# Scores of two heads in float32 on TensorE's row halves, with no split of q and k, and a list schedule that knows the ports shared by VectorE and GpSimd

## The chip, the core and the metric

The kernel runs on one core of one Trainium2 chip. The metric is the device time of one execution in microseconds; less is better. A core has five engines with a queue each: TensorE (PE; its weight loads are shown as PEld), VectorE (DVE), ScalarE (ACT), GpSimd (POOL) and SyncE (SP), which issues the DMAs here.

## What is computed

Sliding-window attention with a linear bias, and behind it a feed-forward part on the attention's output.

```python
# q, k, v: (8 batches, 8 heads, 576 positions, 64)
scores = scale * np.matmul(q, k.transpose(0, 1, 3, 2))
rel = pos[:, None] - pos[None, :]
mask = (rel >= 0) & (rel < 128)
scores = np.where(mask, scores - slopes[h] * np.abs(rel), -1e9)
attn = softmax(scores)
x = (attn @ v).transpose(0, 2, 1, 3).reshape(4608, 512)
h = x @ w_in                                   # 512 -> 2048
g = h * erf(softplus(h))
out = g @ w_out                                # 2048 -> 512
```

Results are wanted at about float32 accuracy. The kernel multiplies some operands as float32 (in the trace one such matmul is two instructions) and others in the rounded type fp32r (one instruction); where fp32r is used, an operand is split into a high and a low part and several products are added.

## The kernel before

**Attention.** There are 32 pairs of heads (8 batches, 4 pairs of heads each). The query positions of a pair are cut into five tiles of 128 (`QTILES`), which see 128, 256, 256, 256 and 192 keys. A "span" is a run of tiles with one load of q and k: tiles 0 to 2, or tiles 3 and 4, and in the later batches both follow from one load. `operands` (L386) loads q and k. `parts` (L439) makes from them what the fp32r products need: for each of the two heads a scaled and rounded k in both row halves (`kh`, L451 on VectorE or L453 on ScalarE), its rest (`kl`, L463, VectorE), the rounded q in the head's own half (`a`, L472 or L474), and q's rest in the other half (L466, GpSimd). So one product of 128 rows adds q-high and q-low at once, and a tile of one head is `a·kh + a·kl`, two fp32r matmuls (L511). The first four spans (`EARLY`) take another way, `early_parts`: q is scaled alone (L435), and each head is one float32 matmul on 64 of the 128 rows (L497).

After the scores, for each tile: VectorE adds the bias and takes the row minimum of the negated scores (L522), ScalarE takes the exponential with its sum (L532), VectorE inverts the sums (L549, L550), GpSimd scales (L560), TensorE transposes by a matmul with the identity (L578), ScalarE or VectorE copies (L472, L474), TensorE multiplies with v in float32 (L596), and the result is copied and stored to DRAM as a chunk of x.

**Feed-forward.** x is cut into 12 chunks of 384 tokens, w_in and w_out into 16 slices of 128 hidden units. A first pass takes slices 0 to 5 over all chunks, beside attention; a second takes the other ten, and adds what the first stored. `Weights.prepare` makes float32 high and low parts out of the weights' 64-bit words (L670 to L692: ScalarE, VectorE and GpSimd). `load_x` splits a chunk (L766 or L768, L759). `unit` (one slice with one chunk) runs 12 fp32r matmuls into a PSUM bank "h" (L782) and copies it out as `hs` (L766, L768); `flush` takes softplus and erf (L811, L813), the product with h (L824) and its split (`gh`; `gl`, L829); `products` runs nine fp32r matmuls into three banks "o" (L844).

**PSUM.** Eight banks: "h" two, "o0" to "o2", and attention's "s", "t" and one for the products with v. One bank "s" holds both heads of a tile.

**The order.** It is made ahead of the run by a list scheduler (`Plan.run`). Each piece of work is an `op` with a cost in us per engine that may do it, the buffers that it reads and writes, and a due time `at`. When an engine is free in the plan, it takes the ready op of the lowest `(at, seq)` whose buffers are to be had. An op that several engines may do goes to the one that ends it first. The order so found is each engine's queue; on the chip each engine runs its queue in order and waits on semaphores, so the planned costs (`dve`, `act`, `pool_tt`, `pool_ts`, `fp32_us`, `f32r_us`) set the order and nothing else. Forty float32 matmuls of no use (`warm_up`, L383) fill TensorE's free time at the start, with the latest due time of all.

Of the kernel before, what the change touches and what calls it, by code (L numbers as in the profile page):

```python
# [8 lines left out]
F32 = mybir.dt.float32  # L9
# [4 lines left out]
ALU = mybir.AluOpType  # L14
# [19 lines left out]
EARLY = 4  # L34
# [6 lines left out]
PB, XB, OB, TB, TBB = 8, 3, 3, 2, 2  # L41
BT = 0
# [90 lines left out]
class Plan:  # L133
# [16 lines left out]
    def op(self, costs, emit, r=(), w=(), at=0.0, moved=0, rows=1.0):  # L150
        o = Op()
        o.rows = rows
# [31 lines left out]
    def run(self):  # L184
# [6 lines left out]
        transfer = 0.0  # L191
# [48 lines left out]
        while events:  # L240
# [17 lines left out]
            for e in ("SP", "PE", "Act", "DVE", "Pool"):  # L258
                while free.get(e, 0.0) <= t + 1e-9 and ready.get(e):
                    best = None  # L260
                    for o in ready[e]:
                        if o.ready > t + self.WAIT[e] + 1e-9 or (best and (best.at, best.seq) < (o.at, o.seq)):
                            continue
                        if fits(o) and all(t + o.costs[e] <= max(free[x], t) + c for x, c in o.costs.items()):
                            best = o
# [36 lines left out]
def dve(n, fast=False):  # L302
    return 0.17 + n * (0.00056 if fast else 0.00108)


def act(n, aps=0, src=0.15):
# [36 lines left out]
class Attention:  # L343


    def __init__(self, tc, plan, ctx, actx, qT, kT, vb, bias, ident, moe):
# [5 lines left out]
        self.raw, self.split, self.pp, self.ptp, self.xsb = (  # L352
            sb(n) for n in ("raw", "split", "pp", "ptp", "xsb")
        )
# [10 lines left out]
        self.seq = 0  # L365
# [20 lines left out]
    def operands(self, i, w=None):  # L386

        nc, op = self.nc, self.plan.op
        sync = nc.sync.dma_start
        b, g = self.order[i]  # L390
        at = step_time(self.step) - LL
        q0, q1 = (0, S) if w is None else SPANS[w][1:3]
        k0 = max(0, q0 - WIN)
        nq, nk = q1 - q0, q1 - k0
        early = self.seq < EARLY
        nm = f"{i}_{w}"
        tags = [("a0", "kh0"), ("a1", "kh1"), ("kl0", "kl1")][self.seq // 2 % 3]
        self.seq += 1
        if early:
            q = Buf(self.split, [P, S], F32, tags[0], 2, "a" + nm)  # L400
            k = Buf(self.split, [P, S], F32, tags[1], 2, "k" + nm)
            op(emit=lambda e: sync(k[:, :nk], self.kT[b, g, :, k0:q1]), w=[k], at=at, **dma(P * nk * 4))
        else:
            q = Buf(self.raw, [P, S], F32, "qr", 1, "qr" + nm)
            k = Buf(self.raw, [P, 2, S], F32, "kr", 1, "kr" + nm)
            src = self.kT[b, g, :, k0:q1].rearrange("(j d) s -> d j s", j=2)

            def both(e):
                for half in range(2):
                    sync(k[half * D : (half + 1) * D, :, :nk], src)  # L410

            op(emit=both, w=[k], at=at, **dma(2 * P * nk * 4, 2, 0.65))
        op(emit=lambda e: sync(q[:, :nq], self.qT[b, g, :, q0:q1]), w=[q], at=at, **dma(P * nq * 4))
        at = step_time(self.step) - LP
        return (*(self.early_parts if early else self.parts)(nm, g, q, k, nq, nk, at), q0, k0)
# [16 lines left out]
    def early_parts(self, nm, g, q, k, nq, nk, at):  # L432
        for j in range(2):
            rows = slice(j * D, (j + 1) * D)
            self.plan.op({"DVE": dve(nq, True)}, lambda e, j=j, rows=rows: self.nc.vector.tensor_scalar(  # L435
                q[rows, :nq], q[rows, :nq], 2.0 ** (2 * g + j), None, op0=ALU.mult), r=[q], w=[q], at=at)
        return q, k, None

    def parts(self, nm, g, q, k, nq, nk, at):  # L439

        nc, op = self.nc, self.plan.op
        lo, hi = slice(0, D), slice(D, P)
        a = [Buf(self.split, [P, S], F32R, f"a{j}", 2, f"a{nm}_{j}") for j in range(2)]
        kh = [Buf(self.split, [P, S], F32R, f"kh{j}", 2, f"kh{nm}_{j}") for j in range(2)]
        kl = [Buf(self.split, [P, S], F32R, f"kl{j}", 2, f"kl{nm}_{j}") for j in range(2)]

        def scaled(e, out, src, by):
            if e == "DVE":  # L450
                nc.vector.tensor_scalar(out, src, by, None, op0=ALU.mult)  # L451
            else:
                nc.scalar.mul(out, src, by)  # L453

        either = lambda n: {"DVE": dve(n, True), "Act": act(n)}
        for j in range(2):
            own, other = (lo, hi) if j == 0 else (hi, lo)
            by = 2.0 ** (2 * g + j)
            op(either(nk), lambda e, j=j, by=by: scaled(e, kh[j][:, :nk], k[:, j, :nk], by),
               r=[k], w=[kh[j]], at=at)  # L460
            op(either(nq), lambda e, j=j, own=own: self.copy(e, a[j][own, :nq], q[own, :nq]),
               r=[q], w=[a[j]], at=at)
            op({"DVE": dve(nk)}, lambda e, j=j, by=by: nc.vector.scalar_tensor_tensor(  # L463
                kl[j][:, :nk], k[:, j, :nk], by, kh[j][:, :nk], op0=ALU.mult, op1=SUB),
                r=[k, kh[j]], w=[kl[j]], at=at)
            op({"Pool": pool_tt(nq)}, lambda e, j=j, own=own, other=other: nc.gpsimd.tensor_tensor(  # L466
                a[j][other, :nq], q[own, :nq], a[j][own, :nq], SUB), r=[q, a[j]], w=[a[j]], at=at)
        return a, kh, kl

# [6 lines left out]
    def scores(self, i, t, operands, low, total, at):  # L476
# [5 lines left out]
        a, kh, kl, q0, k0 = operands  # L482
        k0 = start - WIN + c0 * 64 - k0
        q0 = start - q0
        src = []
        if kl is None:

            ways = [((self.ps, "s", 1), (self.ps, "t", 1))]
            if i < NPAIR and t < 3:
                ways = [((self.ps, "s", 1), (self.spare[1], "o0", 1)), ((self.spare[0], "h", 2),) * 2]  # L490
            for j, (pool, tag, bufs) in enumerate(ways[self.step % len(ways)]):
                src.append((Buf(pool, [P, 2, 256], F32, tag, bufs, f"s{i}_{t}_{j}"), 0))

            def products(e):
                for j in range(2):
                    rows = slice(j * D, (j + 1) * D)
                    nc.tensor.matmul(  # L497
                        src[j][0][:m, src[j][1], :n], lhsT=a[rows, q0 : q0 + m],
                        rhs=kh[rows, k0 : k0 + n], start=True, stop=True,
                    )  # L500

            op({"PE": 2 * fp32_us(n) + 0.05}, products, r=[a, kh], w=[src[0][0], src[1][0]],
               at=at, rows=0.5)
        else:
            ps = Buf(self.ps, [P, 2, 256], F32, "s", 1, f"s{i}_{t}")
            src = [(ps, 0), (ps, 1)]

            def products(e):
                for j in range(2):
                    for o, rhs in enumerate((kh[j], kl[j])):  # L510
                        nc.tensor.matmul(  # L511
                            ps[:m, j, :n], lhsT=a[j][:, q0 : q0 + m], rhs=rhs[:, k0 : k0 + n],
                            start=(o == 0), stop=(o == 1),
                        )

            op({"PE": 4 * f32r_us(n) + 0.05}, products, r=[*a, *kh, *kl], w=[ps], at=at)
# [3 lines left out]
        def biased(e):  # L520
            for j in range(2):
                nc.vector.tensor_tensor_reduce(  # L522
                    out=pt[:m, c0:c1, j, :], in0=blocks(src[j][0][:m, src[j][1], :n]),
# [17 lines left out]
    def normalise(self, i, ts, p, st, totals, at):  # L541
# [11 lines left out]
        op({"DVE": 0.5}, inverse, r=sums, w=sums, at=at)  # L553
# [13 lines left out]
    def transpose_bank(self, i, w, bi, p, sb, at):  # L567
# [18 lines left out]
        op({"DVE": dve(width), "Act": act(width, src=0.13)},  # L586
# [18 lines left out]
    def span(self, i, w, operands, v):  # L605
# [32 lines left out]
        op({"DVE": dve(n), "Act": act(n, src=0.13)},  # L638
# [7 lines left out]
class Weights:  # L646
# [9 lines left out]
    def prepare(self, which, f, at, after=()):  # L656
# [27 lines left out]
        for fast, dst, emit in steps:  # L684
            op({"DVE": dve(DM, fast)}, lambda e, emit=emit: emit(), r=[raw, q, t], w=[dst], at=at)
# [4 lines left out]
            r=[t, *after], w=[hi], at=at)  # L690
        op({"Pool": pool_tt(DM), **({"DVE": dve(DM)} if WLO else {})}, lambda e: (
            nc.gpsimd if e == "Pool" else nc.vector).tensor_tensor(lo.all, flt(t), hi.all, SUB),  # L692
            r=[t, hi, *after], w=[lo], at=at)
# [3 lines left out]
class Moe:  # L697
# [42 lines left out]
    def load_x(self, c, first, at):  # L740
# [11 lines left out]
        for k2 in range(2):  # L752
# [4 lines left out]
               lambda e, hi=hi, src=src: self.copy(e, hi.all, raw[:, src]), r=halves[k2], w=[hi], at=at - XS)  # L757
            op({"Pool": pool_tt(2 * CH), **({"DVE": dve(2 * CH)} if XLO else {})},
               lambda e, hi=hi, lo=lo, src=src: (nc.vector if e == "DVE" else nc.gpsimd).tensor_tensor(  # L759
                   lo.all, raw[:, src], hi.all, SUB), r=[*halves[k2], hi], w=[lo], at=at - XS)  # L760
# [9 lines left out]
    def unit(self, c, f, w, x, po, start, end, first, at):  # L770
# [3 lines left out]
        ps = Buf(self.ps_h, [P, 512], F32, "h", 2, f"h{U}")  # L774
# [16 lines left out]
        op({"Act": act(CH, src=0.13), "DVE": dve(CH)},  # L791
# [3 lines left out]
    def flush(self):  # L795
# [23 lines left out]
        for us, n, n2, hs, s, at in pairs:  # L819
# [5 lines left out]
                r=[s, hs], w=[hs], at=at)  # L825
# [142 lines left out]
```

## Time and profile before

| what | us |
|---|---|
| median of three runs (lowest, highest) | 1118.45 (1116.33, 1119.25) |
| the profiled execution | 1118.25 |
| its span, first to last instruction | 1116.3 |

In the page's line of busy time, a share is of the span. Matmuls are pipelined: a record's length holds the way through the array, so from one start to the next is the better measure of what a matmul costs, and a busy TensorE is not a TensorE at its peak. "PEclk" is the clock that TensorE was granted, in tenths; in this profile it is low only in the first slices, where TensorE has idle time. In a list of groups, the first number after the bar is busy time in us, the second the mean of one in ns, and what follows the second bar is the engine's idle time just before, with what ended it.

### The profile page before, as it was taken

How to read it: one execution, taken by the hardware profiler on the slowest of the kernel's cores; microseconds unless marked ns; L12 is line 12 of the kernel's file. 1: busy time of each engine (PE TensorE's matmuls, PEld its weight loads, DVE VectorE, ACT ScalarE, POOL GpSimd, SP SyncE). 2: the span in 40 equal slices, each digit the busy share in tenths (PEclk: the TensorE clock that was granted, in tenths of full speed). 3: DMA queues.
4: the chain of work that ended last, by engine and by line, in shares of the span. 5: the costliest groups of instructions: out<-in, count | busy, mean ns of one | idle time of the engine just before them, and what ended most of it. 6: DMA issues, size and time to landing. Idle time of an engine off the chain costs nothing.

```text
span 1116.3 us, 17069 instructions
## 1 busy us (share of the span) xinstructions
PE 1073.7 (96%) x6000; PEld 976.5 (87%) x6000; DVE 684.9 (61%) x1602; ACT 721.9 (65%) x1436; POOL 385.7 (35%) x464
## 2 busy tenths in 40 slices
PE   9776979999999999999999999999999999999998
PEld 8666968988899999999899998899999999999996
DVE  5878898887888888775867675333433433433332
ACT  6567667878788787776677675355455455455462
POOL 5776887646666566653333231000000000000000
PEclk9797999999999999999999999999999999999999
DMA  6444555444545455422343422202202202202102
GB/s 184 139 132 122 140 152 153 146 132 115 163 118 135 121 143 149 118 89 78 114 132 114 141 69 74 86 13 73 85 19 67 85 19 67 85 13 73 57 19 67
DMA packets 89732, 111.59 MB, mean 100 GB/s; under 512 B 45744, under 2 KB 59696, under 8 KB 89648
## 3 DMA queue, kind: packets, MB, share of 16 engines
q1 hardware_dynamic: 89648, 110.52, 33.5%
q8 instruction: 47, 0.77, 0.3%
q14 instruction: 37, 0.30, 0.1%
HBM read 82.18 MB, written 28.31 MB: 99 GB/s over the span
## 4 chain that ended last, share of the span: by engine, by line
PE 82%; DVE 9%; POOL 3%; DMA 2%; issue 2%; ACT 2%; POOLq 0%; SPq 0%; DVEq 0%; ACTq 0%
PE o L844 32%; PE h L782 31%; PE px L596 7%; PE s L511 5%; PE t L578 5%; POOL p L560 2%; DMA xr<-xd 2%; DVE p L522 1%; PE warm_ps L383 1%; DVE xl L759 1%; POOL wto L686 1%; DVE hs L824 1%; DVE gl L829 1%; PE s L497 1%; ACT p L532 1%
## 5 line engine op out<-in xcount | busy, mean ns | idle before, releaser
L782 PE MATMUL h<-xh,whi 128*128 128x384 f32 x768 | 262.5, 342 | 0.0
L782 PE MATMUL h<-xl,whi 128*128 128x384 f32 x768 | 259.2, 338 | 1.6 <-DVE xl L759 1.6
L782 PE MATMUL h<-xh,wli 128*128 128x384 f32 x768 | 259.7, 338 | 0.0
L560 POOL TENSOR_SCALAR p<-p,st 128x256 f32<-128x256 f32 (+2 forms) x320 | 194.0, 623 | 128.1 <-DVE st L550 108.1
L844 PE MATMUL o<-who,gh 128*128 128x512 f32 x576 | 228.8, 397 | 0.6 <-DVE ot L768 0.6
L844 PE MATMUL o<-who,gl 128*128 128x512 f32 x576 | 227.6, 395 | 1.2 <-DVE gl L829 1.2
L844 PE MATMUL o<-wlo,gh 128*128 128x512 f32 x576 | 227.3, 395 | 1.2 <-POOL wlo L692 0.7
L766 ACT COPY hs<-h 128x384 f32<-128x384 f32 x137 | 65.3, 477 | 215.1 <-PE h L782 214.6
L532 ACT ACTIVATE p<-p,st 128x256 f32<-128x256 f32 (+2 forms) x320 | 149.0, 468 | 24.5 <-DVE st L522 23.6
L782 PEld LDWEIGHTS h<-xl,whi 128*128 128x128 f32 x768 | 145.2, 189 | 8.7 <-DVE xl L759 2.1
L782 PEld LDWEIGHTS h<-xh,whi 128*128 128x128 f32 x768 | 145.3, 189 | 6.9 <-ACT hs L766 0.2
L782 PEld LDWEIGHTS h<-xh,wli 128*128 128x128 f32 x768 | 144.8, 189 | 0.2 <-POOL wli L692 0.2
L844 PEld LDWEIGHTS o<-who,gl 128*128 128x128 f32 x576 | 108.1, 188 | 25.4 <-DVE gl L829 2.1
L522 DVE CUSTOM_DVE_ANT_0 p<-s,bias_sb 128x256 f32<-128x256 f32 (+2 forms) x320 | 109.4, 378 | 33.4 <-PE s L511 21.6
L768 DVE COPY hs<-h 128x384 f32<-128x384 f32 x55 | 30.4, 554 | 160.8 <-PE h L782 160.8
L844 PEld LDWEIGHTS o<-wlo,gh 128*128 128x128 f32 x576 | 108.5, 188 | 17.9 <-POOL wlo L692 2.2
L844 PEld LDWEIGHTS o<-who,gh 128*128 128x128 f32 x576 | 108.6, 188 | 16.6 <-DVE ot L768 1.5
L824 DVE TENSOR_TENSOR hs<-s,hs 128x768 f32<-128x768 f32 x96 | 95.2, 1016 | 23.4 <-ACT s L813 23.4
L829 DVE TENSOR_TENSOR gl<-hs,gh 128x768 fp32r<-128x768 f32 x96 | 94.6, 989 | 15.5 <-ACT gh L766 14.7
L578 PE MATMUL t<-ident,p 128*128 128x128 f32 x544 | 85.7, 284 | 17.6 <-POOL p L560 11.8
L578 PEld LDWEIGHTS t<-ident,p 128*128 128x128 f32 x544 | 65.6, 147 | 30.4 <-POOL p L560 14.6
L466 POOL TENSOR_TENSOR a_None<-qr_None,a_None 64x576 fp32r<-64x576 f32 x48 | 76.4, 1592 | 25.7 <-DVE a_None L474 20.7
(80 smaller groups left out, 1653.1 us busy)
## 6 DMA issues: line engine op xcount, KB each, us to landing
xr<-xd SPq DMA_DIRECT2D x22, 768.0 KB, 4.3
kr_None<-k_t SPq DMA_DIRECT2D x48, 288.0 KB, 4.2
pd<-ot SPq DMA_DIRECT2D x36, 256.0 KB, 3.7
ot<-pd SPq DMA_DIRECT2D x36, 256.0 KB, 3.0
wri<-w_in SPq DMA_DIRECT2D x16, 512.0 KB, 3.8
wro<-w_out SPq DMA_DIRECT2D x16, 512.0 KB, 3.7
out_dram<-ot SPq DMA_DIRECT2D x32, 256.0 KB, 2.1
qr_None<-q_t SPq DMA_DIRECT2D x24, 288.0 KB, 3.1
```

The source lines that it names most:

```text
L466: op({"Pool": pool_tt(nq)}, lambda e, j=j, own=own, other=other: nc.gpsimd.tensor_tensor(a[j][other, :nq], q[own, :nq], a[j][own, :nq], SU ...
L511: nc.tensor.matmul(ps[:m, j, :n], lhsT=a[j][:, q0 : q0 + m], rhs=rhs[:, k0 : k0 + n], start=(o == 0), stop=(o == 1),)
L522: nc.vector.tensor_tensor_reduce(out=pt[:m, c0:c1, j, :], in0=blocks(src[j][0][:m, src[j][1], :n]), in1=blocks(self.bias[:m, c0 * 64 : c1 ...
L532: nc.scalar.activation(dst, dst, AF.Exp, bias=low[:m, j : j + 1], scale=-1.0, accum_out=total[:m, j : j + 1],)
L560: nc.gpsimd.tensor_scalar(dst, dst, totals[t][:m, j : j + 1], 1.0, op0=ALU.mult, op1=ALU.mult)
L578: nc.tensor.matmul(ps[:, col : col + P], lhsT=p[t][:, kb].rearrange("p j d -> p (j d)"), rhs=self.ident[:, :], is_transpose=True, start=no ...
L596: self.nc.tensor.matmul(dst[:, q0 - base : q1 - base], lhsT=v[:, blk], rhs=sb[sbi][:, off : off + q1 - q0], start=(blk == order[0][0]), st ...
L766: self.nc.scalar.copy(out, src)
L782: nc.tensor.matmul(ps[:, :CH], lhsT=ww[:, cs], rhs=xx[:, k], start=(k2 + k + n == 0), stop=(k2 + k + n == 4),)
L824: V if e == "DVE" else G).tensor_tensor(hs[:, :n], s[:, :n], hs[:, :n], ALU.mult),
L829: V if e == "DVE" else G).tensor_tensor(gl[:, :n], hs[:, :n], gh[:, :n], SUB),
L844: nc.tensor.matmul(po.all, lhsT=g[:, j, cs], rhs=w.all, start=(u["start"] and n == 0), stop=(u["end"] and n == 2),)
```

## The change

Scores: `EARLY`, `early_parts` and `parts` go. Every span loads q and k once, keeps them in float32 (three buffers each), and scales q in one VectorE instruction, by a column `heads` (1 in the first 64 rows, 2 in the others) and by 4^g. Each tile is two float32 matmuls, one head on rows 0 to 63, the other on rows 64 to 127, each into a PSUM bank of its own.

PSUM: attention's "s" has two banks, "h" has one.

Scheduler: an op has a set `shares` of engines on which it uses the ports that VectorE and GpSimd share; all GpSimd work is in it, and VectorE work that is marked `both=True`. In the plan no two of them overlap, and VectorE leaves the turn to a ready GpSimd op with an earlier due time. VectorE is asked a second time after GpSimd. The planned costs have new constants.

```diff
@@ Plan @@
+    def op(self, costs, emit, r=(), w=(), at=0.0, moved=0, rows=1.0, both=False):
+        o.shares = {"Pool", "DVE"} if both else {"Pool"}
...
-            for e in ("SP", "PE", "Act", "DVE", "Pool"):
+            def first(e):
+                best = None
+                for o in ready[e]:
+                    if o.ready > t + self.WAIT[e] + 1e-9 or (best and (best.at, best.seq) < (o.at, o.seq)):
+                        continue
+                    if e in o.shares and ports > t + 1e-9:
+                        continue
+                    if fits(o) and all(t + o.costs[e] <= max(free[x], t) + c for x, c in o.costs.items()):
+                        best = o
+                return best
+            for e in ("SP", "PE", "Act", "DVE", "Pool", "DVE"):
...
+                    if e == "DVE" and e in best.shares and free.get("Pool", 0.0) <= t + 1e-9 and ready.get("Pool"):
+                        other = first("Pool")
+                        if other and other.ready <= t + 1e-9 and (other.at, other.seq) < (best.at, best.seq):
+                            break
...
+                    if e in best.shares:
+                        ports = best.end
@@ planned costs @@
-    return 0.17 + n * (0.00056 if fast else 0.00108)      # dve
+    return 0.14 + n * (0.00054 if fast else 0.00108)
-    return src + 0.093 * aps + n * 0.000833               # act, src 0.15
+    return src + 0.093 * aps + n * 0.00088                # src 0.17
-    return 0.15 + n * 0.0025                              # pool_tt
+    return 0.18 + n * 0.00214
-    return 0.36 + n * 0.00135                             # pool_ts
+    return 0.27 + n * 0.00082
@@ Attention @@
+        self.heads = Buf(sb("heads"), [P, 1], F32, "heads", 1, "heads")
+        for j in range(2):
+            plan.op({"Pool": 0.2}, lambda e, j=j: self.nc.gpsimd.memset(
+                self.heads[j * D : (j + 1) * D], 2.0**j), w=[self.heads], at=-1)
...
+        q = Buf(self.split, [P, S], F32, "q", QB, "q" + nm)
+        k = Buf(self.split, [P, S], F32, "k", QB, "k" + nm)
+        op({"DVE": dve(nq, True)}, lambda e: nc.vector.tensor_scalar(
+            q[:, :nq], q[:, :nq], self.heads[:, 0:1], 4.0**g, op0=ALU.mult, op1=ALU.mult),
+           r=[q, self.heads], w=[q], at=step_time(self.step) - LP, both=True)
-    def early_parts(self, nm, g, q, k, nq, nk, at):
...
-    def parts(self, nm, g, q, k, nq, nk, at):
...
+        ways = [((self.ps, "s", 2),) * 2]
+        if i < NPAIR and t < 3:
+            ways.append(((self.spare[0], "h", 1), (self.spare[1], "o0", 1)))
...
+        def products(e):
+            for j in range(2):
+                rows = slice(j * D, (j + 1) * D)
+                nc.tensor.matmul(
+                    src[j][0][:m, :n], lhsT=q[rows, q0 : q0 + m], rhs=k[rows, k0 : k0 + n],
+                    start=True, stop=True,
+                )
+        op({"PE": 2 * max(n / 1200.0, 0.205) + 0.15}, products, r=[q, k], w=[x[0] for x in src],
+           at=at, rows=0.8)
@@ Moe.unit @@
-        ps = Buf(self.ps_h, [P, 512], F32, "h", 2, f"h{U}")
+        ps = Buf(self.ps_h, [P, 512], F32, "h", 1, f"h{U}")
```

Marked `both=True` are, besides the scaling of q: the inversion of the sums, VectorE's steps in `Weights.prepare`, the split of x, and in `flush` the product with h and the two parts of g.

More of the change, by code (lines that the diff above doesn't have):

```diff
@@ L33 @@
 TAIL = (2, 2)
-EARLY = 4
 DIRECT = 2
@@ L41 @@
 PB, XB, OB, TB, TBB = 8, 3, 3, 2, 2
+QB = 3
 BT = 0
@@ L190, in run @@
         events = []
-        transfer = 0.0
+        transfer = ports = 0.0
         key = lambda b: (id(b.pool), b.tag)
@@ L257, in run @@
                         enable(x, max(late, t))
-            for e in ("SP", "PE", "Act", "DVE", "Pool"):
-                while free.get(e, 0.0) <= t + 1e-9 and ready.get(e):
[L260 to L265, printed above, removed]
+            def first(e):
[9 more added lines that the diff above has]
+            for e in ("SP", "PE", "Act", "DVE", "Pool", "DVE"):
+                while free.get(e, 0.0) <= t + 1e-9 and ready.get(e):
+                    best = first(e)
                     if best is None or best.ready > t + 1e-9:
                         break
+                    if e == "DVE" and e in best.shares and free.get("Pool", 0.0) <= t + 1e-9 and ready.get("Pool"):
+                        other = first("Pool")
+                        if other and other.ready <= t + 1e-9 and (other.at, other.seq) < (best.at, best.seq):
+                            break
                     for x in best.costs:
@@ L351, in __init__ @@
         ps = lambda name: ctx.enter_context(tc.tile_pool(name=name, bufs=1, space=PSUM))
-        self.raw, self.split, self.pp, self.ptp, self.xsb = (
-            sb(n) for n in ("raw", "split", "pp", "ptp", "xsb")
-        )
+        self.split, self.pp, self.ptp, self.xsb = (sb(n) for n in ("split", "pp", "ptp", "xsb"))
         self.ps = ps("ps_a")
@@ L394, in operands @@
         nq, nk = q1 - q0, q1 - k0
-        early = self.seq < EARLY
         nm = f"{i}_{w}"
[L397 to L412, printed above, removed]
+        q = Buf(self.split, [P, S], F32, "q", QB, "q" + nm)
+        k = Buf(self.split, [P, S], F32, "k", QB, "k" + nm)
+        op(emit=lambda e: sync(k[:, :nk], self.kT[b, g, :, k0:q1]), w=[k], at=at, **dma(P * nk * 4))
         op(emit=lambda e: sync(q[:, :nq], self.qT[b, g, :, q0:q1]), w=[q], at=at, **dma(P * nq * 4))
-        at = step_time(self.step) - LP
-        return (*(self.early_parts if early else self.parts)(nm, g, q, k, nq, nk, at), q0, k0)
+        op({"DVE": dve(nq, True)}, lambda e: nc.vector.tensor_scalar(
+            q[:, :nq], q[:, :nq], self.heads[:, 0:1], 4.0**g, op0=ALU.mult, op1=ALU.mult),
+           r=[q, self.heads], w=[q], at=step_time(self.step) - LP, both=True)
+        return q, k, q0, k0
     def values(self, i, c0, c1):
@@ L430, in values @@
         return v
-    def early_parts(self, nm, g, q, k, nq, nk, at):
[L433 to L437, printed above, removed]
-    def parts(self, nm, g, q, k, nq, nk, at):
[L443 to L468, printed above, removed]
     def copy(self, e, out, src):
@@ L481, in scores @@
         n = (c1 - c0) * 64
-        a, kh, kl, q0, k0 = operands
+        q, k, q0, k0 = operands
         k0 = start - WIN + c0 * 64 - k0
         q0 = start - q0
[L485 to L516, printed above, removed]
@@ new lines, in scores @@
+        ways = [((self.ps, "s", 2),) * 2]
+        if i < NPAIR and t < 3:
+            ways.append(((self.spare[0], "h", 1), (self.spare[1], "o0", 1)))
+        src = [
+            (Buf(pool, [P, 512], F32, tag, bufs, f"s{i}_{t}_{j}"), 0)
+            for j, (pool, tag, bufs) in enumerate(ways[self.step % len(ways)])
+        ]
+        def products(e):
[5 more added lines that the diff above has]
+                )
@@ L552, in normalise @@
         sums = [totals[t] for t in ts]
-        op({"DVE": 0.5}, inverse, r=sums, w=sums, at=at)
+        op({"DVE": 0.42}, inverse, r=sums, w=sums, at=at, both=True)
         for t in ts:
@@ L637, in span @@
             xs = Buf(self.xsb, [P, n], F32, f"xs{w}", 1, f"xs{i}_{w}")
-        op({"DVE": dve(n), "Act": act(n, src=0.13)},
+        op({"DVE": dve(n), "Act": act(n, src=0.145)},
            lambda e: self.copy(e, xs.all, px[:, :n]), r=[px], w=[xs], at=at + 0.1)
@@ L684, in prepare @@
         for fast, dst, emit in steps:
-            op({"DVE": dve(DM, fast)}, lambda e, emit=emit: emit(), r=[raw, q, t], w=[dst], at=at)
+            op({"DVE": dve(DM, fast)}, lambda e, emit=emit: emit(), r=[raw, q, t], w=[dst], at=at, both=True)
         op({"Pool": pool_tt(DM)}, lambda e: nc.gpsimd.tensor_tensor(flt(t), flt(t), flt(q), ALU.add),
@@ L689, in prepare @@
             nc.scalar.copy if e == "Act" else nc.vector.tensor_copy)(hi.all, flt(t)),
-            r=[t, *after], w=[hi], at=at)
+            r=[t, *after], w=[hi], at=at, both=True)
         op({"Pool": pool_tt(DM), **({"DVE": dve(DM)} if WLO else {})}, lambda e: (
             nc.gpsimd if e == "Pool" else nc.vector).tensor_tensor(lo.all, flt(t), hi.all, SUB),
-            r=[t, hi, *after], w=[lo], at=at)
+            r=[t, hi, *after], w=[lo], at=at, both=True)
         self.t[which, f] = (hi, lo)
@@ L756, in load_x @@
             op({"DVE": dve(2 * CH, True), "Act": act(2 * CH)},
-               lambda e, hi=hi, src=src: self.copy(e, hi.all, raw[:, src]), r=halves[k2], w=[hi], at=at - XS)
+               lambda e, hi=hi, src=src: self.copy(e, hi.all, raw[:, src]), r=halves[k2], w=[hi], at=at - XS, both=True)
             op({"Pool": pool_tt(2 * CH), **({"DVE": dve(2 * CH)} if XLO else {})},
                lambda e, hi=hi, lo=lo, src=src: (nc.vector if e == "DVE" else nc.gpsimd).tensor_tensor(
-                   lo.all, raw[:, src], hi.all, SUB), r=[*halves[k2], hi], w=[lo], at=at - XS)
+                   lo.all, raw[:, src], hi.all, SUB), r=[*halves[k2], hi], w=[lo], at=at - XS, both=True)
             x.append((hi, lo))
@@ L790, in unit @@
         hs, half = self.hs, len(self.round) % 2
-        op({"Act": act(CH, src=0.13), "DVE": dve(CH)},
+        op({"Act": act(CH, src=0.145), "DVE": dve(CH)},
            lambda e: self.copy(e, hs[:, half], ps[:, :CH]), r=[ps], w=[hs], at=at)
@@ L858, in store @@
         if u["first"]:
-            op({"DVE": dve(DM), "Act": act(DM, src=0.13)},
+            op({"DVE": dve(DM), "Act": act(DM, src=0.145)},
                lambda e: self.copy(e, ot.all, po.all), r=[po], w=[ot], at=at)
```

14 lines of the change are left out of this document (6 added, 8 removed).

## The prediction

> **What bounds the kernel now.** I read the page's busy shares first, then its 40 slices and the chain, then the windows by stage, and only then single groups and the order of time on TensorE.
>
> ```profile
> PE 1073.7 (96%) x6000; PEld 976.5 (87%) x6000; DVE 684.9 (61%) x1602; ACT 721.9 (65%) x1436; POOL 385.7 (35%) x464
> PEclk9797999999999999999999999999999999999999
> PE 82%; DVE 9%; POOL 3%; DMA 2%; issue 2%; ACT 2%; POOLq 0%; SPq 0%; DVEq 0%; ACTq 0%
> 20.00:200.00 180.00, 149.72 (x884) 135.58 (x884) 151.02 (x423) 123.71 (x331) 135.68 (x157) 0.90 0.52 143
> 200.00:520.00 320.00, 315.01 (x2041) 292.70 (x2039) 251.13 (x763) 255.10 (x648) 186.72 (x249) 1.00 0.44 125
> 600.00:1117.00 517.00, 511.45 (x2560) 462.10 (x2558) 211.76 (x281) 277.40 (x350) 27.80 (x20) 1.00 0.19 63
> ```
>
> The window columns are busy time of PE, PEld, DVE, ACT, POOL, then the granted clock. TensorE carries 82% of the chain, but not evenly. From 20 to 200 us it is busy 149.7 of 180 us, idle 30.3, at a granted clock of 0.90; VectorE is busy 151.0 (84%), ScalarE 123.7 (69%), GpSimd 135.7 (75%). From 200 to 520 us TensorE is busy 315.0 of 320 at full clock. After 600 us there is only the feed-forward part, and TensorE is never free. So work taken from the other engines pays before 200 us; work given to TensorE costs after 200 us. The change does both, and the forecast is their difference.
>
> **The change part by part.** Times are made against the profiled execution, 1118.25 us (span 1116.3, about 2 us around it); the median of the three runs, 1118.45, is 0.2 above.
>
> *1. The splits of q and k go.* These groups, all between 20 and 200 us, fall away:
>
> ```profile
> L463 DVE SCALAR_TENSOR_TENSOR kl<-kr,kh 128x320 fp32r<-128x320 f32 (+1 forms) x22 | 11.6, 547 | 1.9 <-ACT kh L453 1.8
> L463 DVE SCALAR_TENSOR_TENSOR kl_None<-kr_None,kh_None 128x576 fp32r<-128x576 f32 x10 | 7.9, 792 | 0.0
> L451 DVE TENSOR_SCALAR kh<-kr 128x320 fp32r<-128x320 f32 (+1 forms) x14 | 6.5, 492 | 1.8 <-DMA kr<-k_t 1.8
> L451 DVE TENSOR_SCALAR kh_None<-kr_None 128x576 fp32r<-128x576 f32 x5 | 3.1, 625 | 0.2 <-PE s L511 0.2
> L474 DVE CAST a<-qr 64x192 fp32r<-64x192 f32 (+1 forms) x11 | 4.6, 421 | 3.3 <-DMA qr<-q_t 3.2
> L474 DVE CAST a_None<-qr_None 64x576 fp32r<-64x576 f32 x7 | 3.9, 558 | 0.0
> L453 ACT ACTIVATE kh<-kr 128x320 fp32r<-128x320 f32 x8 | 3.5, 466 | 2.1 <-PE s L511 1.7 <-DMA kr<-k_t 0.4
> L453 ACT ACTIVATE kh_None<-kr_None 128x576 fp32r<-128x576 f32 x5 | 3.4, 673 | 0.0
> L472 ACT CAST a<-qr 64x192 fp32r<-64x192 f32 (+1 forms) x11 | 4.3, 394 | 1.1 <-DMA qr<-q_t 1.0
> L472 ACT CAST a_None<-qr_None 64x576 fp32r<-64x576 f32 x3 | 2.0, 672 | 0.1
> L466 POOL TENSOR_TENSOR a<-qr,a 64x192 fp32r<-64x192 f32 (+1 forms) x24 | 22.5, 936 | 13.5 <-DVE wqi L678 4.2 <-DVE a L474 3.1 <-ACT a L472 2.2
> L466 POOL TENSOR_TENSOR a_None<-qr_None,a_None 64x576 fp32r<-64x576 f32 x10 | 16.3, 1632 | 3.1 <-DVE a_None L474 2.5
> ```
>
> VectorE loses 11.6+7.9+6.5+3.1+4.6+3.9 = 37.6 us, ScalarE 3.5+3.4+4.3+2.0 = 13.2, GpSimd 22.5+16.3 = 38.8. Added is one VectorE scaling of q per span. GpSimd's 34 instructions were two a span, so 17 spans; at about 0.45 us (the casts of q took 0.42 to 0.56 on half the partitions) that is 7.7 us. VectorE goes from 151.0 to 121.1, ScalarE from 123.7 to 110.5, GpSimd to 96.9. Many copies may run on VectorE or ScalarE, and the planner hands them out, so I take the two together: 274.7 becomes 231.6, a factor 0.843. If they stay as loaded as now, the stage takes 0.843 × 180 = 152 us: **28 us** less. VectorE alone would give 144, ScalarE alone 161, which are the inner bounds. TensorE's floor is about 141: 149.7 us of busy time at clock 0.90 is 135 at full clock, and part 2 adds some 6. Then 39 us would be gained; nothing gained is the other end, if the stage is a chain of waits and not a load.
>
> The second load of k (two transfers become one) leaves the SP queue and is costed at nothing: no transfer stands on the chain for more than the 2% named above.
>
> *2. Scores as two float32 products on row halves.* The first four spans of before already do exactly this, at L497, so the price is in the trace.
>
> ```profile
> 14.52 1.14 PE L497 MATMUL s<-k,a 64*128 64x256 f32 x8
> 15.59 1.16 PE L383 MATMUL warm_ps<-warm 128*128 128x128 f32 x8
> 17.77 0.49 PE L497 MATMUL s<-k,a 64*128 64x128 f32 x4
> 18.19 1.96 PE L596 MATMUL px<-pa,vbd 128*128 128x192 f32 x12
> 20.71 1.31 PE L578 MATMUL t<-ident,p 128*128 128x128 f32 x10
> 21.95 0.70 PE L497 MATMUL s<-k,a 64*128 64x256 f32 x4
> 22.59 1.96 PE L596 MATMUL px<-pa,vbd 128*128 128x192 f32 x12
> 24.35 0.31 PE L511 MATMUL s<-kh,a 128*128 128x128 f32 x1
> 24.83 1.55 PE L383 MATMUL warm_ps<-warm 128*128 128x128 f32 x12
> 26.14 0.36 PE L511 MATMUL s<-kh,a 128*128 128x256 f32 x1
> 26.70 1.25 PE L578 MATMUL t<-ident,p 128*128 128x128 f32 x10
> L511 PE MATMUL s<-kl_None,a_None x206: 272/278/285, 199.9 to 509.4; 128*128 128x256 f32 x62, 128*128 128x192 f32 x21, 128*128 128x128 f32 x20
> ```
>
> Columns are start and length. From its first matmul to the next group's first, a 256-wide tile on row halves takes 22.59−21.95 = 0.64 us, against 26.70−26.14 = 0.56 for the four fp32r products; a 128-wide one 18.19−17.77 = 0.42 against 24.83−24.35 = 0.48. There is a price ahead of it too. The ten transposes at 26.70 span 1.25 us, of which the last matmul's own record is about 0.27, so they start 0.11 apart. The ten at 20.71 end at 22.02, so the last began near 21.75, and the row halves begin 0.20 later: 0.09 of wait that the fp32r products do not have (26.14 follows a last warm-up start near 26.11). So the row halves cost 0.73 and 0.51. If the early start of the fp32r group is credited too (0.08), that form costs 0.48. The extra is 0.17 to 0.25 for a 256-wide tile; I take 0.19, near the row without credit. For 128 wide I take 0.05, for 192, which no row shows, 0.11 between them.
>
> From 200 to 520 us the last row gives 62, 21 and 20 tiles: 62×0.19 + 21×0.11 + 20×0.05 = **15 us**, all on a TensorE that is 98% busy. Over the whole kernel (88, 32 and 28 tiles that still split) it is 22 us; the rest falls into the early idle time and is inside part 1. The lower end is two tiles in a row, 15.59−14.52 = 1.07 us, or 0.58 each with the wait ahead: 0.02 extra, 1 to 2 us in the stage. But the two PSUM banks "s" hold one tile, so two in a row is not what will stand there.
>
> The Trainium skill, "TensorEngine Tiling (Array Packing)", section Tiling Modes, says that a change of tiling mode drains TensorE; it speaks against this change. The trace agrees, with 0.09 us ahead of the group, and by that rule every isolated tile pays, as the sum has it; without the rule it would be the 0.02 above.
>
> *3. One PSUM bank "h" instead of two* (the second now holds scores).
>
> ```profile
> 720.17 0.33 PE L782 MATMUL h<-xh,wli 128*128 128x384 f32 x1
> 720.34 0.39 PE L844 MATMUL o<-who,gh 128*128 128x512 f32 x1
> 720.54 0.48 ACT L766 COPY hs<-h 128x384 f32<-128x384 f32 x1 [2.55 <-PE h L782]
> 722.42 0.33 PE L782 MATMUL h<-xh,whi 128*128 128x384 f32 x1
> 651.62 7.30 PE h L782 x42
> 667.27 5.24 PE h L782 x30
> ```
>
> In the steady part the copy ends at 721.02 and the next h starts at 722.42: nine o products lie between, 1.4 us to spare, so the second bank is not used and nothing changes in the last 400 us. The cover is those o products. Where h units stand back to back (the last two rows of the chain, 42 and 30 matmuls at 12 a unit) it is gone: each next unit then waits 0.37 + 0.48, some 0.9 us, and everything on TensorE behind it, unless o, transposes or scores are ordered between. Between nothing and 0.9 × 72 units of the first pass = 65 us; I take **4 us**, nearest the steady rows, as some five units in a row here and there.
>
> *4. Plan costs and the port rule.* They change the order of work alone; nothing in it makes an engine wait.
>
> ```profile
> L560 POOL TENSOR_SCALAR p<-p,st x320: 364/475/3002, 12.4 to 514.6; 128x256 f32<-128x256 f32 x96, 128x128 f32<-128x128 f32 x32, 128x192 f32<-128x192 f32 x32
> L675 DVE SCALAR_TENSOR_TENSOR wti<-wqi,wti x16: 677/691/1784, 32.1 to 588.9; 128x512 int32<-128x512 int32 x16
> L675 DVE SCALAR_TENSOR_TENSOR wti<-wqi,wti 128x512 int32<-128x512 int32 x7 | 8.8, 1264 | 0.1
> ```
>
> The same instruction takes 0.68 or 1.78 us on VectorE, 0.36 to 3.0 on GpSimd; the seven early ones average 1.26, so they lost 7×(1.26−0.69) = 4 us. Some of that comes back because GpSimd has less to do, some if the order holds. I take nothing beyond part 1 and keep up to 5 us for the low end. It could also lose: the order is made for planned times.
>
> After 200 us TensorE has 5 us of idle time; with lighter engines beside it I give back 3. The sum: −28 + 15 + 4 − 3 = **−12**, so **1106 us**, with 1097 to 1113 as this case's own range.
>
> **The rivals.**
>
> *A. TensorE's price decides: slower.* Two rows of TensorE's waits before 200 us speak for it:
>
> ```profile
> PE t L578 <- POOL p L560: 11.8, 7, 5.4
> PE s L511 <- DVE st L522: 11.1, 9, 2.0
> ```
>
> Of the 30 us that TensorE is idle from 20 to 200 us, 23 end with the softmax chain, none with a split. If that chain's length and not the load sets the pace, only some 7 us come back (30−23), while the 15 stay and the single h bank, in ten units without o between, costs 9: 1118 − 7 + 15 + 9 = 1135. It decides as soon as the early stage returns less than about 16 us. Against it: the chain's steps queue behind the splits on VectorE and GpSimd, which are loaded 84% and 75%.
>
> *B. The drain is hidden and the early stage closes to TensorE's floor:* −39 + 2 − 3 + 1 = −39, near 1079. For it: the clock returns with the idle time. Against: every isolated L497 group shows the drain.
>
> *C. A wash:* VectorE's relief only lets ScalarE become the bound (161 us, 19 less), and 15 + 4 go back: 1118. The port rule not holding on the chip would look alike.
>
> **How the numbers follow.** Forecast 0.45, A 0.24, B 0.15, C 0.16. What a measurement here can tell from no change is about 0.3%, or 3.4 us. C puts 0.08 within it and 0.04 on each side; the forecast's upper edge gives 0.03 to "same". Faster 0.45 − 0.03 + 0.15 + 0.04 = 0.61, same 0.11, slower 0.28. The range leaves half of B and half of A out (0.195): 1086 to 1134.
>
> **What would show it.** Part 1: PE idle from 20 to 200 us falls from 30 towards 10 and half-clock slices vanish; if VectorE's share there falls and PE's idle does not, A. Part 2: row-half tiles among fp32r work cost 0.7 us by the next group's start; 0.5 makes it B. Part 3: PE waiting for "hs" on VectorE or ScalarE is new; more than 10 us of it makes the forecast wrong. Part 4: GpSimd's 623 ns mean at L560 should near its median. A later start of feed-forward work than in before would overturn all of it.

## The result, and the profile after

The changed kernel takes 1125.67 us (median of four runs, 1125.09 to 1126.95), the kernel before 1118.04 in the same comparison: 1.0071 times as long, with a 95% interval of 1.0053 to 1.0088. It is slower by about 8 us. The forecast was 1106.

The page of the changed kernel, its busy shares, the granted clock and the chain, and then its windows by stage (busy time of PE, PEld, DVE, ACT, POOL, then the clock):

```profile
PE 1101.1 (98%) x6000; PEld 944.5 (84%) x6000; DVE 612.6 (54%) x1547; ACT 653.1 (58%) x1302; POOL 250.9 (22%) x399
PEclk9998999999999999999999999999999999999999
PE 94%; DVE 2%; ACT 1%; POOL 1%; issue 1%; DMA 0%; POOLq 0%; DVEq 0%; ACTq 0%
```

```profile
20.00:200.00 180.00, 166.86 (x993) 134.61 (x992) 130.25 (x439) 118.68 (x325) 90.63 (x138) 0.97 0.46 138
200.00:520.00 320.00, 319.78 (x1917) 258.99 (x1916) 193.43 (x677) 203.95 (x536) 98.37 (x202) 1.00 0.31 96
```

What was hoped for before 200 us happened. TensorE's idle time from 20 to 200 us fell from 30.3 us to 180 − 166.86 = 13.1, the clock there rose from 0.90 to 0.97, and of the chain TensorE now has 94% where it had 82%. Yet the kernel is slower. From 200 to 520 us TensorE is busy all the time and starts 1917 matmuls where it started 2041; a tile's scores are four records in both kernels, and there is less of every kind of work: 380 score matmuls where there were 410, 441 for h where there were 468, 327 for o where there were 352. So it does less in the same time.

To separate the two, I took every matmul's start-to-start time over the whole trace, and split it: idle time before the next one; of the rest, the part that the granted clock took (the rest times one minus the clock); and what remains, TensorE's own time (in every kernel it holds some 6 us of the span that lie before the first matmul and behind the last). Spans and parts in us:

| kernel | span | idle | clock | TensorE's own time |
|---|---|---|---|---|
| before | 1116.3 | 36.8 | 15.7 | 1063.8 |
| changed | 1124.3 | 17.6 | 4.8 | 1101.9 |

Idle and clock gave back 30.1; TensorE's own time grew by 38.1. The difference is the 8 us. The expectations further down have these parts as 24 (idle and clock in the changed kernel) and 37 (the growth): taken over the whole span, its idle time and end included, the changed kernel's lower clock makes 6.0 us instead of 4.8.

Where it grew is seen in order of time. First a tile of 256 in the kernel before, then two tiles in the changed one (start, length):

```profile
303.42 0.36 PE L511 MATMUL s<-kh_None,a_None 128*128 128x256 f32 x1
303.62 0.28 PE L511 MATMUL s<-kl_None,a_None 128*128 128x256 f32 x1
303.74 0.28 PE L511 MATMUL s<-kh_None,a_None 128*128 128x256 f32 x1
303.86 0.28 PE L511 MATMUL s<-kl_None,a_None 128*128 128x256 f32 x1
303.98 0.34 PE L782 MATMUL h<-xh,whi 128*128 128x384 f32 x1
304.15 0.34 PE L782 MATMUL h<-xl,whi 128*128 128x384 f32 x1
```

```profile
303.43 0.33 PE L737 MATMUL h<-xl,whi 128*128 128x384 f32 x1
303.61 0.34 PE L737 MATMUL h<-xh,wli 128*128 128x384 f32 x1
303.88 0.70 PE L465 MATMUL s<-k_None,q_None 64*128 64x256 f32 x4
304.51 0.50 PE L799 MATMUL o<-who,gh 128*128 128x512 f32 x1
304.84 0.39 PE L799 MATMUL o<-wlo,gh 128*128 128x512 f32 x1
305.07 0.39 PE L799 MATMUL o<-who,gl 128*128 128x512 f32 x1
...
313.05 0.49 PE L465 MATMUL s<-k_None,q_None 64*128 64x128 f32 x4
313.47 0.45 PE L737 MATMUL h<-xh,whi 128*128 128x384 f32 x1
313.75 0.34 PE L737 MATMUL h<-xl,whi 128*128 128x384 f32 x1
313.93 0.35 PE L737 MATMUL h<-xh,wli 128*128 128x384 f32 x1
```

Read starts, not lengths. In the changed kernel h matmuls start 0.18 apart (303.43, 303.61), but the row halves follow after 0.27: 0.09 ahead. They take 0.63 to the next start. And then the first o matmul holds the second one back: 304.51 to 304.84 is 0.33, where the next step is 0.23, so 0.10 is lost **behind** the visit too. The same stands behind the 128-wide tile: 0.28 (313.47 to 313.75), then 0.18. In the kernel before, h goes on at 303.98 and 304.15, at its usual spacing: nothing is lost.

Over all undisturbed groups (no idle time, full clock), from where the matmul before would usually have been followed to the next group's first start:

| tile | four fp32r products, before: median (mean) | row halves, changed: median (mean) |
|---|---|---|
| 128 wide | 0.40 (0.41) | 0.52 (0.52) |
| 192 wide | 0.43 (0.45) | 0.62 (0.64) |
| 256 wide | 0.48 (0.50) | 0.73 (0.74) |

Behind the visit, before the second h or o matmul, 0.11 is lost in the changed kernel and 0.02 in the one before, by the means. TensorE's weight-load queue shows it as waits for nothing visible ("issue"; in total, times, longest), of which the kernel before has 0.2 us at o and none at h:

```profile
PEld s L465 <- issue: 19.1, 77, 1.6
PEld o L799 <- issue: 13.4, 45, 0.3
PEld h L737 <- issue: 10.5, 35, 0.3
```

The weight loads around the visit at 303.88 show what the loss behind it is; the last row is the load behind the scores of the kernel before, at 303.86:

```profile
303.87 0.30 PEld L465 LDWEIGHTS s<-k_None,q_None 64*128 64x128 f32 x4 [0.25 <-issue]
304.50 0.19 PEld L799 LDWEIGHTS o<-who,gh 128*128 128x128 f32 x1 [0.33 <-issue]
```

```profile
303.86 0.19 PEld L782 LDWEIGHTS h<-xh,whi 128*128 128x128 f32 x1
```

In the kernel before, the load for the first h starts 0.12 ahead of its matmul (303.98), beside the matmul before it. In the changed kernel the load for the first o starts together with its matmul (304.50 and 304.51), and so does the first load of the row halves (303.87 and 303.88). The first o then has a record of 0.50, the next one 0.39: the 0.10 is a weight load that nothing hides. Over the undisturbed groups the medians say the same: 0.002 us from the load to the first h or o behind a visit, 0.11 in the kernel before.

### The profile page after: what moved, and what is told of

It reads as the page before. It is cut to its first block, busy times and chain, and to the rows that moved or that the text cites. A ratio compares the mean times of both kernels' runs of the same rounds, so it can differ in the third digit from the quotient of the medians.

```text
span 1124.3 us, 16558 instructions
## 1 busy us (share of the span) xinstructions
PE 1101.1 (98%) x6000; PEld 944.5 (84%) x6000; DVE 612.6 (54%) x1547; ACT 653.1 (58%) x1302; POOL 250.9 (22%) x399
## 4 chain that ended last, share of the span: by engine, by line
PE 94%; DVE 2%; ACT 1%; POOL 1%; issue 1%; DMA 0%; POOLq 0%; DVEq 0%; ACTq 0%
PE h L737 36%; PE o L799 36%; PE px L551 8%; PE s L465 7%; PE t L533 5%; PE warm_ps L399 1%; POOL p L515 1%; DMA xd<-xs 0%; DVE p L477 0%; DVE gl L784 0%; ACT p L487 0%; ACT hs L721 0%; POOL wto L641 0%; POOLq L919 0%; DVE st L504 0%
## 5 line engine op out<-in xcount | busy, mean ns | idle before, releaser
L737 PE MATMUL h<-xh,whi 128*128 128x384 f32 x768 | 268.4, 349 | 4.2 <-ACT hs L721 3.5
L799 PE MATMUL o<-who,gh 128*128 128x512 f32 x576 | 232.6, 404 | 0.0
L515 POOL TENSOR_SCALAR p<-p,st 128x256 f32<-128x256 f32 (+2 forms) x320 | 150.2, 487 | 269.3 <-DVE st L505 134.0
L721 ACT COPY hs<-h 128x384 f32<-128x384 f32 x121 | 57.9, 479 | 259.4 <-PE h L737 259.0
L723 DVE COPY hs<-h 128x384 f32<-128x384 f32 x71 | 39.5, 557 | 206.5 <-PE h L737 206.2
L779 DVE TENSOR_TENSOR hs<-s,hs 128x768 f32<-128x768 f32 x93 | 89.0, 983 | 24.9 <-ACT s L768 24.9
L784 DVE TENSOR_TENSOR gl<-hs,gh 128x768 fp32r<-128x768 f32 x95 | 91.0, 975 | 3.2 <-ACT gh L721 3.1
L533 PE MATMUL t<-ident,p 128*128 128x128 f32 x544 | 83.2, 279 | 4.4 <-POOL p L515 2.0
L465 PE MATMUL s<-k_None,q_None 64*128 64x256 f32 (+2 forms) x480 | 77.0, 396 | 1.8 <-DVE q_None L417 1.3
```

Of the source, the lines that this page charges most:

```text
L465: nc.tensor.matmul(src[j][0][:m, :n], lhsT=q[rows, q0 : q0 + m], rhs=k[rows, k0 : k0 + n], start=True, stop=True,)
L515: nc.gpsimd.tensor_scalar(dst, dst, totals[t][:m, j : j + 1], 1.0, op0=ALU.mult, op1=ALU.mult)
L533: nc.tensor.matmul(ps[:, col : col + P], lhsT=p[t][:, kb].rearrange("p j d -> p (j d)"), rhs=self.ident[:, :], is_transpose=True, start=no ...
L721: self.nc.scalar.copy(out, src)
L723: self.nc.vector.tensor_copy(out, src)
L737: nc.tensor.matmul(ps[:, :CH], lhsT=ww[:, cs], rhs=xx[:, k], start=(k2 + k + n == 0), stop=(k2 + k + n == 4),)
```

## The experiments

"Own time" is TensorE's, worked out as above; ratios are against the kernel before on the same chip.

**The price of the row halves taken away, all else of the change kept.**

```diff
-                    src[j][0][:m, :n], lhsT=q[rows, q0 : q0 + m], rhs=k[rows, k0 : k0 + n],
-                    start=True, stop=True,
+                for o in range(2):
+                    nc.tensor.matmul(
+                        src[j][0][:m, :n], lhsT=q[:, q0 : q0 + m], rhs=self.kc[:, k0 : k0 + n],
+                        start=(o == 0), stop=(o == 1),
...
```

> The changed kernel, but a tile's scores are four fp32r matmuls over all 128 rows, as many and as wide as in the kernel before, on the scaled q and a constant in place of k (so the scores are left out; loads, scaling and all else stay). Theory (the price of the row halves on TensorE, 37 us from start to start over the kernel, is what turned the gain into a loss): 1125.7 - 37 = 1089 us, between 1083 and 1097, with TensorE's idle and half-clock loss still about 24 us. Rival 1 (the new order costs the time) and rival 2 (the single bank h does): those stay in this kernel, so 1105 or more.

1091.67 us, 0.9764 (0.9748 to 0.978); own time 1060.3, idle and clock 29.9. So all of the change but the row halves gains 26 us, and the row halves cost 34 us on top of it. The rivals, which put the loss on the new scheduler or on the bank, are out: both stand in this kernel. (The planned price of the scores, and with it some of the order, is that of fp32r here.)

**The changed scheduler alone, on the kernel before; and the scheduler of before on the changed kernel.**

```diff
+        o.shares = {"Pool", "DVE"} if both else {"Pool"}   # with the rule and the new costs, in before
```

> The kernel before with the changed scheduler alone: port rule, second turn of VectorE, new planned costs; splits, fp32r scores and two banks h stay. Theory: the order is worth little, 1118 us within 6. Rival 1 (the new order costs): 1125 or more. If the port rule is itself a gain: 1112 or less, with GpSimd's mean at its scaling near 490 ns where it was 623.

1150.3 us, 1.0295 (1.0271 to 1.032): not the theory but rival 1, a loss of 32 us. Own time is 1065.1, as before; idle and clock are 87.4 where they were 52.5. The rule did keep the two engines apart, as far as GpSimd's scaling shows it: its mean is 501 ns, and 597 with the new costs but no rule (the run without the rule, below). First before, then with the new scheduler (the number after the busy time is the mean in ns):

```profile
L560 POOL TENSOR_SCALAR p<-p,st 128x256 f32<-128x256 f32 (+2 forms) x320 | 194.0, 623 | 128.1 <-DVE st L550 108.1 <-ACT p L532 16.4 <-ACT xh L766 1.4
```

```profile
L573 POOL TENSOR_SCALAR p<-p,st 128x256 f32<-128x256 f32 (+2 forms) x320 | 153.9, 501 | 135.7 <-DVE st L563 106.0 <-DVE st L562 17.8 <-ACT p L545 9.6
```

40 us of GpSimd's time came back at this step and bought nothing.

> The changed kernel with the scheduler and planned costs of before (the price of the row-half scores in the plan stays). Theory: 1125.7 us within 5, as the row halves' price stays. Rival 1: 1118 or less.

1126.15 us, 1.0069 (1.0053 to 1.0086), the same as the changed kernel: with the splits gone, the order is not what costs.

> The kernel before with the new planned costs and without the port rule (which cost 32 us together, at 1150). Theory (keeping the loaded VectorE and GpSimd apart is what costs): 1118 within 8. Rival (the new costs do, as they promise GpSimd faster than it is when VectorE is in its way): 1140 or more.

```diff
-        o.shares = {"Pool", "DVE"} if both else {"Pool"}
+        o.shares = set()
```

1158.39 us, 1.0377 (1.0347 to 1.0407). The rival has it: without the rule it is even slower, so what hurts the kernel before is in the new planned costs, and the rule gives a little back. (VectorE's second turn stands in both runs and was not tried alone.) Two rows of TensorE's waits:

```profile
PE t L591 <- POOL p L573: 22.6, 24, 3.4
PE s L524 <- DVE st L535: 13.2, 9, 5.1
```

The transposes wait for GpSimd's scaling 24 times (7 times and 11.8 us in the kernel before), 11 of the 31 us by which TensorE's idle time grew. The new costs also move work between engines. The 96 products with h in `flush` were all VectorE's; now 47 of them are GpSimd's, where one takes twice as long (first before, then this run):

```profile
L824 DVE TENSOR_TENSOR hs<-s,hs 128x768 f32<-128x768 f32 x96 | 95.2, 1016 | 23.4 <-ACT s L813 23.4
```

```profile
L837 POOL TENSOR_TENSOR hs<-s,hs 128x768 f32<-128x768 f32 x47 | 97.2, 2068 | 382.9 <-ACT s L826 367.5 <-issue 14.9
```

With the rule in force GpSimd has five of them. By the new `pool_tt` such a product of 768 columns costs GpSimd 0.18 + 768 × 0.00214 = 1.82 us, by the old one 2.07, which is what it takes (2.068). This fits costs that promise a faster GpSimd than it is; which of the new constants does the harm, and whether it does it by this move, was not tried.

**One bank h in the kernel before.** Two runs, since the first four spans' scores need other banks then:

```diff
-        ps = Buf(self.ps_h, [P, 512], F32, "h", 2, f"h{U}")
+        ps = Buf(self.ps_h, [P, 512], F32, "h", 1, f"h{U}")
-                ways = [..., ((self.spare[0], "h", 2),) * 2]
+                ways = [..., ((self.spare[0], "h", 1), (self.spare[1], "o1", 1))]
```

> The kernel before with one bank h instead of two (the first four spans' second pair of score banks becomes h and o1). Theory, as the prediction had it: 4 us more, 1119 to 1125. Rival 2 (the bank is the loss): 1126 or more. Nothing lost: 1116 to 1119.

1142.43 us, 1.0218 (1.02 to 1.0236): 24 us, as rival 2 had it. TensorE now waits at h for copies of hs, which it does not in the kernel before:

```profile
PE h L782 <- ACT hs L766: 8.8, 10, 3.1
```

> The kernel before with two banks h, but with the banks for the first four spans' scores as in the run with one h (the second pair is h and o1). If the 24 us of that run come from the single bank h: 1116 to 1124. If from the early banks: 1135 or more.

1129.4 us, 1.0098 (1.0069 to 1.0127), between the two answers: 11 of the 24 come with the other early banks, 13 with the single bank or the order that it brings. The waits for hs (8.8 us, and 0.7 more for copies on VectorE) are not in this run, so they can be most of the 13. Own time is 1064 in both; all of it is idle time and clock.

**Two banks h without the row halves.**

```diff
-        ways = [((self.ps, "s", 2),) * 2]
+        ways = [(self.ps, "s", 1)]                       # both heads in one bank
-        ps = Buf(self.ps_h, [P, 512], F32, "h", 1, f"h{U}")
+        ps = Buf(self.ps_h, [P, 512], F32, "h", 2, f"h{U}")
```

> The earlier run with four fp32r matmuls over all rows (1091.7 us, scores left out), now with both heads' scores in one bank s and two banks h, as PSUM was before. In that run TensorE waits some 6 us for copies of hs. Theory (with the splits gone the single bank costs little): 1085 to 1092. Rival (the single bank is worth as much as the 24 us that it cost the kernel before): 1075 or less.

1103.37 us, 0.9868 (0.9854 to 0.9883): above both answers, 12 us slower than with one bank. Own time is lower by 4 (1056.7 against 1060.3), idle and clock are 43.8 against 29.9. One row of TensorE's waits makes half of that, a single wait for a prepared weight:

```profile
PE o L802 <- ACT who L646: 7.2, 1, 7.2
```

TensorE's waits for copies of hs (4.1 and 1.7 us with one bank) are gone, but the second bank h came with one bank s less and with another order, and the sum is a loss. So this run does not price the bank alone. What it shows is that a new order can move some 10 us of idle time, and that is the scale below which the two runs with the early banks cannot be read.

**What the price hangs on.** The row halves in one pass, and float32 without row halves (the line of the product in each of the two runs):

```diff
+                    src[j][0][:m, :n], lhsT=q[rows, q0 : q0 + m], rhs=self.kc[rows, k0 : k0 + n],  # fp32r halves
+                    src[j][0][:m, :n], lhsT=q[:, q0 : q0 + m], rhs=k[:, k0 : k0 + n],              # float32, all rows
```

> The changed kernel with its row-half scores as fp32r (one pass, on the scaled q and a constant in place of k; the scores are left out). Theory (a fixed price per visit for the change between 128 and 64 rows): the streaming falls by some 0.3 us for a 256-wide tile and less for the others, 44 us in all, and the visit's price of about 0.2 to 0.3 us a tile stays: 1082 us, between 1072 and 1092. Rival (the wait belongs to float32 and not to the row halves): fp32r halves would cost half of the four fp32r products before, 0.24 us a tile, and the time falls to about 1050.

1093.84 us, 0.9789 (0.9765 to 0.9812); 2 us above the theory's range and 44 from the rival's. In order of time (start, length):

```profile
305.97 0.39 PE L470 MATMUL s<-kc,qr_None 64*128 64x256 f32 x2
306.29 0.44 PE L742 MATMUL h<-xh,whi 128*128 128x384 f32 x1
306.57 0.33 PE L742 MATMUL h<-xl,whi 128*128 128x384 f32 x1
306.74 0.34 PE L742 MATMUL h<-xh,wli 128*128 128x384 f32 x1
```

Two fp32r matmuls of 256 columns, side by side, hold TensorE for 0.32 from their start to the next group's; in the kernel before four in a row took 0.56 (303.42 to 303.98). By the table's measure, which counts the wait ahead, the median is 0.41 against 0.48: two side by side in place of four in a row gain 0.07. Behind them is the same loss, 0.28 and then 0.17, and ahead of them the same 0.09. Row halves pay the price in either type.

> The changed kernel with each head's float32 product over all 128 rows (both heads' rows summed, so the scores are left out): no row halves, twice the columns in a row. Theory (the change of rows costs): no wait at either end, 1088 columns x 2 heads / 600 = 3.63 us a pair of heads against 3.55 measured on the halves, so 1128 us, between 1120 and 1136, though TensorE streams twice as long. Rival (going from fp32r to float32 and back costs the same wait): 0.2 to 0.3 us a tile more on top, 1155 or more.

1119.75 us, 1.0022 (1.0008 to 1.0035): 0.25 us below the theory's range, far from the rival's, and 6 us **faster** than the row halves, though TensorE streams twice the columns one after another. Of the 6 us some 2 are TensorE's own time (1099.8 against 1101.9), the rest is idle time and clock. The theory's "no wait at either end" held only ahead; the loss behind is in the last section. By the medians a 128-wide tile takes 0.37 where the halves take 0.52, 192 wide 0.52 where they take 0.62; only at 256 are the halves ahead, 0.73 against 0.86.

**Fewer visits.** If the price is paid per visit, two tiles in one visit save it; the second tile goes behind the first in the same two banks.

```diff
+        groups, src = {0: (0, 1), 2: (2,), 3: (3, 4)}, {}
...
+            for off, n, a, b in where.values():
+                for j in range(2):
+                    rows = slice(j * D, (j + 1) * D)
+                    nc.tensor.matmul(banks[j][:P, off : off + n],
+                        lhsT=q[rows, a : a + P], rhs=k[rows, b : b + n], start=True, stop=True)
```

> The changed kernel with the row-half scores of two tiles in one go (tiles 0 and 1, 2, 3 and 4; the second tile behind the first in the same two banks): three visits of TensorE to the row halves for each pair of heads where the changed kernel has five. Theory (the price is paid per visit: the wait at the change of rows ahead of it, and a first weight load that nothing hides): a 256-wide tile alone costs 0.72 to 0.85 us in the changed kernel, two in a row 1.16, so a pair of heads costs about 2.8 us where it cost 3.55; 32 x 0.75 = 24 less, 1102 us, between 1095 and 1110, below the kernel before. Rival (the price is paid per matmul): 1126 within 4.

1104.34 us, 0.9882 (0.9864 to 0.9899): faster than both kernels, and close to the 1102 expected. Own time is 1077.3, 24.6 below the changed kernel's. A visit with tiles 3 and 4:

```profile
308.46 0.72 PE L539 MATMUL t<-ident,p 128*128 128x128 f32 x5
309.10 1.03 PE L462 MATMUL s<-k_None,q_None 64*128 64x256 f32 x8
310.06 0.44 PE L539 MATMUL t<-ident,p 128*128 128x128 f32 x2
```

From 309.10 to 310.06, 0.96 us, it does what took 0.63 and 0.52 in two visits, and the waits ahead and behind are paid once. By the table's measure (medians) a visit with tiles 0 and 1 takes 0.95 and one with tiles 3 and 4 takes 1.05, where the tiles alone take 0.52 + 0.73 and 0.73 + 0.62. With 0.1 saved behind each, that is 0.8 us for a pair of heads and 26 us for 32, near the 24.6 measured.

> Two tiles a visit (1104 us) without the port rule, the new planned costs kept. Theory (with the splits gone the rule is worth little, as the changed kernel with the old scheduler showed): 1104 within 6, with GpSimd's mean at its scaling back from below 500 ns to about 570. Rival (the rule pays once TensorE has less to do): 1112 or more.

1104.22 us, 0.9887 (0.9865 to 0.9908): the same without the port rule (`o.shares = set()`, as above). The plan again gives GpSimd 47 of the 96 products with h, and here it costs nothing. GpSimd's mean went up less than expected, from 497 to 540 ns:

```profile
L521 POOL TENSOR_SCALAR p<-p,st 128x256 f32<-128x256 f32 (+2 forms) x320 | 166.3, 540 | 155.9 <-DVE st L511 63.0 <-ACT p L493 20.4 <-PE px L557 18.2
```

## Why the prediction was wrong

**1. The splits go: right.** In the forecast's own terms, idle time and clock were to fall by 33 us (28 in the early stage, 6 more of new TensorE work hidden there, 3 later, less 4 for the bank); they fell by 30.1. The run without row halves gains 26 us by the same load. This step is some 3 of the 20 us between forecast and result.

**2. The row halves: this step failed, by its size.** It gave 22 us over the kernel and 15 of them where nothing hides them; TensorE's own time grew by 38.1, and that is some 16 of the 20 us. The price of a row-half tile itself was read rightly (0.73 and 0.51, measured 0.73 and 0.52). Two other terms were wrong, and the rows quoted there had both. First, the extra of a 256-wide tile was taken as 0.19, "near the row without credit", from bounds of 0.17 to 0.25. The credit was real: the fp32r products start early behind transposes (by 0.08) and wait for nothing behind h and o, so the medians give 0.73 − 0.48 = 0.25, and likewise 0.12 and 0.19 where 0.05 and 0.11 were taken. By the means, which hold the fp32r groups' stragglers, it is 28 × 0.11 + 32 × 0.19 + 88 × 0.23 = 29 us. Second, the price behind the visit had no term. Eight warm-ups at 15.59 spanned 1.16 us; at 0.112 apart with a last record of 0.28 they should have spanned 1.06. The 0.10 stood in a quoted row and was not read. The loss behind averages about 0.10 a visit in the changed kernel and 0.02 in the one before; 148 visits at the difference, 0.08, give about 12 us. Together 41, against 38.1 measured. The lower end, two tiles in a row at 0.02 extra, was dismissed because of the banks; the run with two tiles in one bank came near it (0.95 and 1.05 a visit against 0.88 and 0.91 for the fp32r tiles, 0.04 to 0.07 a tile).

The Trainium skill, "TensorEngine Tiling (Array Packing)", section Tiling Modes, says that switching the mode drains TensorE. The runs agree: the wait is there on both sides for row halves in either type. Here it is a wait of about 0.1 us ahead, and on each side a first weight load that starts only with its matmul; the one behind is the 0.1 us lost there.

**3. One bank h: about right here.** 4 us were given; in the changed kernel TensorE waits 3.5 and 0.7 us at h for copies of hs by its list of waits:

```profile
PE h L737 <- ACT hs L721: 3.5, 6, 0.7
PE h L737 <- DVE hs L723: 0.7, 1, 0.7
```

In the loaded kernel before, the waits for hs alone are 9.5 us and the bank goes with 13 to 24, so the 4 seems to have held because the load had gone; no run shows that by itself.

**4. Scheduler: right that it is worth nothing here,** with the splits gone (1126.15 and 1104.22 without the rule, 1125.67 and 1104.34 with it). GpSimd's mean at its scaling did fall to near its median, from 623 to 487 ns, and bought nothing. What the new costs do on the loaded kernel, 32 us more with the rule and 41 without, was not foreseen.

**The rivals.** A had the right side and the right price as its cause, but needed the early stage to return little; the early stage returned nearly all that was forecast, and the price itself was larger. B's floor was not reached in any run with row halves. C's "port rule not holding" was not it.

**Left open:** which planned cost turns the kernel before to 1158, and how much of the 13 us in the run with one bank h is the order's, beyond the 9.5 of waits for hs.

## What to carry to other kernels

Price an operation that changes TensorE's row mode per visit, from the usual spacing of what stands ahead to the *second* start behind it, and compare it with the old form measured the same way. Half-width work that is scattered among full-width work can lose at its edges all that it gains side by side; gather it into fewer visits before judging it. When work leaves the engines beside a saturated one, only the idle time of the saturated engine comes back, and any time added to it is paid in full.

## What the runs showed of the hardware that was not expected

- Row halves among full rows start 0.09 to 0.10 us late where they follow transposes, h or o, 0.15 late where they follow the float32 products with v, and hold back the second matmul behind them by 0.11 (0.06 where that is a transpose), in float32 and fp32r alike.
- Float32 over all rows waits for nothing behind transposes, h or o, but the second fp32r matmul behind it loses about 0.15 by the means, and 0.20 in these rows: h at 302.40 and 302.77, then 302.94.

```profile
301.73 1.03 PE L464 MATMUL s<-k_None,q_None 128*128 128x256 f32 x4
302.40 0.53 PE L735 MATMUL h<-xh,whi 128*128 128x384 f32 x1
302.77 0.34 PE L735 MATMUL h<-xl,whi 128*128 128x384 f32 x1
302.94 0.34 PE L735 MATMUL h<-xh,wli 128*128 128x384 f32 x1
```

- New planned costs (with VectorE's second turn), over the same work, moved the kernel before from 1118 to 1158 us; 54 pieces of the feed-forward part changed from VectorE to GpSimd on the way.
